# A spectral filter with a gated feed-forward branch: the gate and up products of the last row block as seven block products, and the schedule written anew

## The chip, the cores and the metric

The kernel runs on one core of a Trainium2 chip. A core has TensorE (PE, matrix products), VectorE (DVE), ScalarE (ACT), GpSimd (POOL) and SyncE (SP, which issues most transfers); each works through its own queue in the order in which it was written, and waits on semaphores for the others. Matrix products leave their sums in PSUM, from which VectorE and ScalarE read. The metric is the device time of one execution in microseconds, as the median of several runs.

## The reference

```python
xn = _layernorm(x, axis=-1)              # x: 2048 rows of 512
X = rfft2(xn); y = irfft2(X * (w_r + 1j * w_i), (S, D))      # s
gate = einsum("bsd,df->bsf", xn, W_gate) # 512 -> 1376
up   = einsum("bsd,df->bsf", xn, W_up)
h = gate * (gate > 0) * up
g = silu(einsum("bsf,fd->bsd", h, W_down))
return x + s * g
```

So there are two branches over the same normalised rows: a two-dimensional Fourier filter (s) and a feed-forward branch whose output is a gate (g). All values are 32-bit.

## The kernel before

Every 32-bit operand of a product is split into a high and a low 16-bit part, and each product is made in three passes (high by high, high by low, low by high; the list is PASSES). The 2048 rows stand as 16 tiles of 128. Eight chunks of two tiles (index c or q, 0 to 7) carry the loading and the Fourier branch; four row blocks of 512 rows (c = 0 to 3) carry the feed-forward branch. The 1376 features are 11 tiles (index f): ten of 128 and a last one of 96.

For a row block and a feature tile `product` makes gate or up: 12 matmuls of 128 weights by 512 rows (four slices of the 512 inputs, three passes) into a PSUM tile gu{c}_{f}_{0 or 1}. `rectify` (ScalarE) takes the positive part of gate into r, `hidden` multiplies it with up on VectorE (h32), takes the high part on ScalarE and the low part on VectorE (h16). `down` adds three matmuls of one feature tile to the PSUM tile dn{c}_{i} of row tile i; `gate` makes g from it on ScalarE. `weights` of the products are loaded in seven groups (`load_group`), scaled and split (`group_split`) in the first 60 us or so. The scale of the down weights needs the greatest value over all partitions, which goes to DRAM and back (row_md, rows_md).

The Fourier branch of a chunk is a chain over all engines: fold and split (eo, ee, xs), first stage (s, t), to DRAM (A_d), back with rows exchanged (at), then y, a, xx, the filter (xsp, tt on VectorE, po and pf as sums of tt on POOL, p), z, v, again to DRAM (C_d) and back (ct), a second stage s2 (zz on ScalarE, ae on POOL, ye and sv on VectorE). `finish` multiplies sv with g, adds the rows of x that were loaded again (xt) and stores out.

All steps are given to the class `Plan` with their engine, an estimated cost, what they read and write, and for some a due time. Plan's `run` walks in its own estimated time, gives every engine the most urgent step whose inputs are there, counts tiles of each kind of buffer (k4, k2, xg, gu, dn and so on), and so sets the order in which each engine's instructions are written. The order is then kept by the chip; the estimates are used for nothing else. The due times of the Fourier stages are the lists at the head of the file (FIRSTS, MIDS, LASTS); those of the products come from a running clock (`tick`). From `ff_steps`: a down step follows its product by six feature tiles.

Of the kernel before, what the change touches and what calls it, by code (L numbers as in the profile page):

```python
# [14 lines left out]
P = 128  # L15
# [10 lines left out]
TAIL = NFT - 1  # L26

# [5 lines left out]
T0, DOWN, FILTER, TICK = 1.2, 93.937, 134.179, 1.169  # L33
FIRSTS = [53.32, 98.69, 53.46, 108.61, 118.2, 143.13, 197.12, 178.58]
MIDS = [150.3, 160.34, 188.08, 192.0, 219.21, 237.31, 253.81, 275.45]
STAGES = [0, 12.12, 20.71, 25.24]
LASTS = [286.02, 290.71, 285.79, 312.67, 324.45, 353.1, 333.77, 342.56]
ENDS = [21.7, 8.89]
LOADS, LOADX = [-0.52, -0.11, 3.18, None, None, None, None], [-30, -0.3]
FOLDS, FOLD_LEAD, MARGIN = ['DVE', 'DVE', 'DVE', 'DVE', 'DVE', 'DVE', 'DVE', 'DVE'], 97.974, 1.95  # L40
HIGH_ACT = {(0, 1), (2, 1), (0, 0), (3, 1), (2, 0), (3, 0)}
NORM, TURN1 = (('DVE', 'ACT'), ('DVE', 'ACT')), 'PE'
YCOST, VCOST, SCOST, MODE, JOIN = 0.63, 0.59, 0.6, 0.095, 21.31
BUSY, LATE = 42, 0.4
SQUARES, HALF = 43.857, 2
HURRY, SLOW, SLOW_TO = -2.352, 1, 20
LOWS = [("DVE", "DVE")] * 8
ALONE, EVAC, WHOLE = (((0,), (1,)), ((0, 1),)), ("ACT", "DVE"), .95
HALVES, HEADS, STATS = ('gu', 'F'), [None, 13.67], ((0, 1),)
RATE, SLACK, TURNKB = 320, .6, 1300  # L50
LEADS = [None, 6.55, 6.95, 7.64, 6.43, 6.38, 7.22]
# [29 lines left out]
class Plan:  # L81
# [47 lines left out]
    def run(self):  # L129
        steps = self.steps  # L130
        for s in reversed(steps):
            s.due = 1e9 if s.due is None else s.due
            for d in s.deps:
                t = s.due - d.cost - d.lag
                d.due = t if d.due is None else min(d.due, t)
        base = lambda n: n[0] if isinstance(n, tuple) else n
# [9 lines left out]
        dma, todo, order, mode = 0., {e: [] for e in free}, [], 0  # L146
# [7 lines left out]
        for _ in steps:  # L154
            best = None
            for e, mine in todo.items():
# [16 lines left out]
                if at:  # L173
# [9 lines left out]
                    if best is None or t < best[0]:  # L183
                        best = t, s
# [13 lines left out]
            if s.kb:  # L198
                if s.block:
                    s.end = free[e] = max(s.end, dma + s.block)  # L200
                dma = max(dma, s.end) + s.kb / (340 if t < 40 else RATE)
                s.end = dma + (SLACK if t > 40 else 0.)
            if s.port:
                ports[e] = s.end
# [32 lines left out]
def pool(n):  # L237
    return .26 + n / 600
# [7 lines left out]
def kernel(ctx: ExitStack, tc: tile.TileContext, x, wg, wu, wd, wl, ew, sp, c_r, c_d, c_m, c_x, c_s, out):  # L246
# [14 lines left out]
    E_d = dram.tile([2, 2, 1024], F32, name="E_d")  # L261

# [6 lines left out]
    wgu = [wpool.tile([P, 2, 2, 4, P * sum(f < TAIL for f in g)], F16, name=f"wgu{i}") for i, g in enumerate(GROUPS)]  # L269
    wgt = wpool.tile([P, 4, 3, P], F16, name="wgt")  # L270
# [7 lines left out]
    md = cpool.tile([P, NFT + 1], F32, name="md")  # L278
    sc = cpool.tile([P, NFT], F32, name="scd")
# [11 lines left out]
    T = Plan({"k4": 12, "k2": 10, "h16": NFT, "xg": NBL + 1, "F": 2, "gu": 2, "dn": 2, "q": 4, "q4": 2, "mv": 4, "m": 4, "p": 4, "am": 1, "mid": 3})  # L291
# [34 lines left out]
    def stats(c, q, j):  # L326
# [6 lines left out]
        tile_of(f"mv{c}", "mv", [P, 2, 2], F32)  # L333
        if c == 0:
            tile_of(f"xf{c}", "k4", [P, 2, D + 2], F32)
        for i in range(2):
            if (c, i) in STATS:
# [38 lines left out]
    def deviations(cs):  # L376
# [15 lines left out]
        step("DVE", 2.4, run, reads=[(f"mv{c}", i) for c in cs for i in range(2)], writes=[(name, 2)], port=True)  # L392

    def normalise(c, q, at, engines=("DVE", "DVE")):
# [3 lines left out]
        def run(i):  # L398
            to, x = T[f"xf{c}"][:, i, 0:D], T[f"x{c}"][:, i, :]
            if engines[i] == "ACT":  # L400
                ACT.activation(to, x, AF.Identity, bias=T[q][:, 0, i:i + 1], scale=at()[:, i:i + 1])
            else:
                DVE.tensor_scalar(to, x, T[f"mv{c}"][:, i, 0:1], at()[:, i:i + 1], op0=ALU.subtract, op1=ALU.mult)
        for i in range(2):
            e = engines[i]
            step(e, .62 if e == "ACT" else dve2(512), lambda i=i: run(i), reads=[*x_names(c, i), (f"mv{c}", i), (q, 2, i) if c < 2 else (q, 2)],
                 writes=[(f"xf{c}", i)], port=e == "DVE")

    def turn(c, lows):
# [844 lines left out]
```

## Time and profile before

| | us |
|---|---|
| runs shown, median (lowest to highest of 3) | 407.4 (406.66 to 407.64) |
| the profiled execution | 406.56 |
| its span, first to last instruction | 404.8 |
| busy: TensorE | 398.4 (98%) |
| busy: VectorE | 305.0 (75%) |
| busy: ScalarE | 190.8 (47%) |
| busy: GpSimd | 50.4 (12%) |
| moved by DMA | 51.79 MB |

The trace is of one execution. A group of its rows is one kind of instruction: output and inputs by the program's names, shape, count, then the busy time and the mean duration of one in ns, then the time that the engine idled ahead of it and who ended that. For TensorE the mean duration holds the pipeline's latency and is not the pace; the pace is read from the chain of work that ended last, where a piece is its start, its length and the count of its instructions. The profile's page cuts the span into 40 slices of 10.1 us; another view gives each engine's busy time between two times. All rows of helper functions bear one line number.

### The profile page before, as it was taken

To read this page: it belongs to the slowest core of one execution; us is meant where nothing else is said; L and a number is where in the kernel's file an instruction comes from. 1 tells how busy PE (TensorE), PEld (TensorE's weight loads), DVE (VectorE), ACT (ScalarE), POOL (GpSimd) and SP (SyncE) were. 2 spreads that over 40 slices of the span, in tenths; PEclk is the share of its full clock that TensorE was granted. 3 is DMA by queue.
4 is the path that set the end of the run, shared out by engine and by line. 5 is a ranking of instruction groups with operands and counts; after the bars stand their busy time and mean duration, and the time that the engine had idled before them with its cause. 6 is when DMAs were issued, how large, how long until landed. Compare 5 with 4: busy or idle time off the path is not lost.

```text
span 404.8 us, 7658 instructions
## 1 busy us (share of the span) xinstructions
PE 398.4 (98%) x3004; PEld 211.2 (52%) x3004; DVE 305.0 (75%) x656; ACT 190.8 (47%) x368; POOL 50.4 (12%) x72
## 2 busy tenths in 40 slices
PE   8999999999999999999999999999999999999996
PEld 7854445444444444455565455546555445544446
DVE  4989898998699998327867568787872326889874
ACT  6989753454566753131444435424533236451211
POOL 0000000000000000004212014030330006516000
PEclk9999999999999999999999999999999999999999
DMA  7992000352099967930006450172102498433342
GB/s 256 401 324 80 0 2 7 105 108 101 12 276 289 278 33 201 255 119 2 2 0 187 162 160 2 25 223 95 51 5 52 122 237 215 157 104 106 104 157 104
DMA packets 36436, 51.79 MB, mean 128 GB/s; under 512 B 15856, under 2 KB 17744, under 8 KB 36400
## 3 DMA queue, kind: packets, MB, share of 16 engines
q1 hardware_dynamic: 36400, 51.31, 44.0%
q8 instruction: 23, 0.38, 0.4%
q14 instruction: 13, 0.11, 0.1%
HBM read 35.55 MB, written 12.60 MB: 119 GB/s over the span
## 4 chain that ended last, share of the span: by engine, by line
PE 89%; DMA 5%; DVE 4%; ACT 1%; issue 0%; POOL 0%; DVEq 0%
PE gu L74 49%; PE dn L74 28%; PE z L74 3%; PE xx L74 3%; PE s L74 3%; DMA row_md<-md 2%; DMA x<-in_x 2%; PE y L74 2%; PE v L74 2%; DMA rows_md<-row_md 1%; PE dn_3bb L74 0%; PE dn_3b L74 0%; ACT wgu L74 0%; DVE eo L74 0%; ACT xT L74 0%; DVE xT L74 0%
## 5 line engine op out<-in xcount | busy, mean ns | idle before, releaser
L74 PE MATMUL gu<-xT,wgu 128*128 128x512 f16 (+1 forms) x960 | 208.3, 374 | 1.1 <-DVE h L74 0.6
L74 PEld LDWEIGHTS <-wgu 128*128 128x128 f16 x960 | 93.0, 98 | 107.2 <-issue 3.9
L74 PE MATMUL dn<-wds,h 128*128 128x512 f16 (+2 forms) x528 | 116.0, 373 | 0.5 <-DVE wds L74 0.5
L74 PEld LDWEIGHTS <-h 128*128 128x128 f16 (+1 forms) x594 | 54.3, 98 | 57.9 <-issue 3.0
L74 ACT ACTIVATE h<-h 128x512 f16<-128x512 f32 (+1 forms) x44 | 27.4, 627 | 58.5 <-DVE h L74 58.4
L74 DVE TENSOR_TENSOR h<-gu,r 128x512 f32<-128x512 f32 (+3 forms) x52 | 33.1, 636 | 27.1 <-PE gu L74 25.3
L74 POOL TENSOR_TENSOR po<-tt,tt 128x256 f32<-128x256 f32 x16 | 13.8, 864 | 262.5 <-DVE tt L74 249.1
L74 ACT ACTIVATE r<-gu 128x512 f32<-128x512 f32 (+2 forms) x44 | 25.7, 583 | 38.4 <-PE gu L74 35.6
L74 DVE TENSOR_TENSOR h<-h,h 128x512 f16<-128x512 f32 (+1 forms) x44 | 29.9, 696 | 7.1 <-ACT h L74 7.0
L74 POOL TENSOR_TENSOR ae<-zz 128x128 f32<-128x128 f32 (+1 forms) x32 | 21.2, 696 | 49.9 <-ACT zz L74 39.6
L74 DVE SCALAR_TENSOR_TENSOR tt<-xsp,cw,wt 128x512 f32<-128x512 f32 x32 | 25.9, 864 | 0.0
L74 ACT ACTIVATE g<-dn,cdi 128x512 f32<-128x512 f32 (+1 forms) x16 | 10.6, 672 | 25.5 <-PE dn L74 25.5
L74 DVE TENSOR_TENSOR z<-z,z 128x1024 f16<-128x1024 f32 x8 | 9.8, 1223 | 11.0 <-ACT z L74 11.0
L74 PE MATMUL gu<-xT,wgt 128*64 128x256 f16 (+1 forms) x144 | 17.0, 310 | 0.0
L74 DVE TENSOR_TENSOR a<-y,a 128x1024 f16<-128x1024 f32 x8 | 9.8, 1219 | 8.7 <-ACT a L74 8.7
L74 DVE TENSOR_TENSOR t<-v,t 128x1024 f16<-128x1024 f32 x8 | 9.7, 1219 | 8.6 <-ACT t L74 8.6
L74 POOL TENSOR_TENSOR pf<-tt,tt 128x256 f32<-128x256 f32 x16 | 14.8, 941 | 4.9 <-issue 3.6
L74 DVE TENSOR_TENSOR sv<-sv,g 128x512 f32<-128x512 f32 (+2 forms) x18 | 11.0, 648 | 5.3 <-ACT g L74 5.2
L74 DVE SCALAR_TENSOR_TENSOR wgu<-raw,p,wgu 128x512 f16<-128x512 f32 x20 | 14.2, 746 | 0.8 <-ACT wgu L74 0.7
L74 ACT ACTIVATE a<-y 128x1024 f16<-128x1024 f32 x8 | 8.1, 1022 | 13.8 <-PE y L74 13.8
L74 ACT ACTIVATE z<-z 128x1024 f16<-128x1024 f32 x8 | 8.2, 1021 | 13.3 <-PE z L74 13.3
L74 DVE TENSOR_TENSOR p<-pf,p 128x1024 f16<-128x1024 f32 x8 | 9.8, 1225 | 5.6 <-ACT p L74 5.6
(151 smaller groups left out, 447.2 us busy)
## 6 DMA issues: line engine op xcount, KB each, us to landing
A_d<-t SPq DMA_DIRECT2D x16, 256.0 KB, 4.3
rw<-in_wl SPq DMA_DIRECT2D x8, 512.0 KB, 5.2
wt<-in_wl SPq DMA_DIRECT2D x8, 512.0 KB, 4.9
at<-A_d SPq DMA_DIRECT2D x8, 512.0 KB, 4.2
C_d<-t SPq DMA_DIRECT2D x16, 256.0 KB, 3.2
ct<-C_d SPq DMA_DIRECT2D x16, 256.0 KB, 6.8
xt<-in_x SPq DMA_DIRECT2D x16, 256.0 KB, 4.1
out<-xt SPq DMA_DIRECT2D x15, 256.0 KB, 2.1
```

What stands on the lines that cost most here:

```text
L74: return lambda *args, **kw: self.tc.keep_in_program_order(f(*args, **kw))
```

## The change

For the last row block, four of the five pairs of feature tiles ((0, 1), (5, 6), (7, 8) and (2, 9)) no longer make 2 × 2 products of 12 matmuls by 512 rows. Their gate and up, taken as a product of 2 by 2 blocks (two halves of the rows, two halves of the inputs), come from seven block products of 12 matmuls by 256 columns, `mult` in `fast_products`. Three PSUM tiles (A, B, C; sa, sb, sc by name) hold partial sums; ScalarE copies A to B and C to `back` (sk), VectorE adds B and back to C and E (se). The rest is as in rectify and hidden, on half-row tiles h16_3_n_m.

This needs sums of weight blocks and of row blocks. `weight_sums` loads the raw weights of a pair again, scales them on ScalarE, makes four differences on VectorE, splits them (wT), and writes one of them over part of the up weights in wgu. `row_sums` makes four sums of the normalised rows of block 3, splits them and sends them through DRAM to be transposed (xS).

Beside that: the normalised rows of chunks 4 to 7 go through DRAM to their transpose (X_d) instead of straight from on-chip memory. g of blocks 0 to 2 goes to DRAM (G_d) and is loaded again in `finish`. In `finish`, chunks 0, 1, 3 and 4 copy x to out in DRAM and add s times g to it with an accumulating transfer that POOL issues; the others load xt and add on VectorE as before. The row statistics of chunks 2 and 4 to 7 go to ScalarE; more high parts of weights too (HIGHS); half of POOL's sums go to VectorE (SUM2, DIFF2). There are fewer buffers of most kinds (ROOM) and three for gu. Feature tiles go in pairs, with the down steps two pairs behind, and single rows of down in block 0. The planner's costs and all due times are new.

```diff
-T0, DOWN, FILTER, TICK = 1.2, 93.937, 134.179, 1.169
-FIRSTS = [53.32, 98.69, 53.46, 108.61, 118.2, 143.13, 197.12, 178.58]
+T0, DOWN = 1.2, 98.707
+FIRSTS = [31.43, 109.07, 105.79, 129.3, 181.09, 150.51]
...
+PAIRS = ((0, 1), (3, 4), (5, 6), (7, 8), (2, 9))
+STATS, ADDS, COPIES = ['DVE', 'DVE', 'ACT', 'DVE', 'ACT', 'ACT', 'ACT', 'ACT'], ['DMA', 'DMA', 'DVE', 'DMA', 'DMA', 'DVE', 'DVE', 'DVE'], [105.83, 259.66, 138.19, 267.03, 599.36, 405.66, 358.32, 606.44]
+SUM2, DIFF2 = ['POOL', 'POOL', 'DVE', 'POOL', 'DVE', 'DVE', 'POOL', 'DVE', 'POOL', 'DVE', 'DVE', 'POOL', 'POOL', 'DVE', 'DVE', 'POOL'], ['DVE', 'POOL', 'POOL', 'POOL', 'POOL', 'DVE', 'DVE', 'DVE', 'POOL', 'DVE', 'POOL', 'DVE', 'POOL', 'DVE', 'DVE', 'POOL']
+ROOM = {"k4": 10, "k2": 8, "kg": 4, "cm": 3, "h16": 11, "xg": 3, "F": 2, "gu": 3, "dn": 1, "q": 4, "q4": 2, "mv": 4, "m": 4, "p": 4, "am": 1, "mid": 3}
-    T = Plan({"k4": 12, "k2": 10, "h16": NFT, "xg": NBL + 1, "F": 2, "gu": 2, "dn": 2, "q": 4, "q4": 2, "mv": 4, "m": 4, "p": 4, "am": 1, "mid": 3})
+    T = Plan(ROOM)
...
-            SP.dma_start_transpose(xt.rearrange("p i k r -> p (i k) r"), x16().rearrange("p i h d -> p (i h d)"))
+            SP.dma_start_transpose(xt.rearrange("p i k r -> p (i k) r"), x16().rearrange("p i h d -> p (i h d)") if DIRECT[c] else X_d[c])
...
+    def weight_sums(n, due):
...
+                step("SP", .5, lambda i=i, j=j, of=of, o=o: SP.dma_start(T[raw][:, i, :, j * P:j * P + P], of[:, :, o:o + P]),
+                     reads=["go"], writes=[(raw, i, j)], lead=8, kb=330, due=due - 12)
+                part = lambda i=i, j=j: T[raw][:, i, :, j * P:j * P + P]
+                step("ACT", act(512) + .1, lambda part=part, f=f, i=i: ACT.activation(part(), part(), AF.Copy, scale=csc[:, i, f:f + 1]),
+                     reads=[("csc", f)], writes=[(raw, i, j)])
...
+        minus((0, 0), (1, 0), (0, 0), G + U, t1)
+        minus((1, 0), (1, 1), (1, 0), U + [t1], t3)
+        minus((1, 1), (1, 1), (0, 0), U + [t1, t3], t2)
+        minus((0, 1), (0, 1), (1, 1), G + [t2], t4)
...
+    def fast_products(c, n):
...
+        def mult(to, x, w, fresh, reads):
+            def run():
+                for j in range(2):
+                    for k in range(2):
+                        for p, (h, l) in enumerate(PASSES):
+                            matmul(T[to][:, j, :], w(h, k, j), x(l, k), start=fresh and j == k == p == 0, stop=j == k == 1 and p == 2, skip_group_check=True)
+            step("PE", pe(12, 256), run, reads=reads, writes=[to, "turn"], due=tick(pe(12, 256)), margin=FMARGIN)
...
+        mult(A, rows(0, 0), plain(0, 0), True, X[0] + W[0])
+        copy(B, A)
+        mult(C, rsum(2), plain(1, 0), True, [(f"xS{c}", 1)] + W[1])
+        copy(back, C)
+        mult(B, rsum(1), summed(2), False, [(f"xS{c}", 0)] + U(2, 3))
+        mult(A, rows(0, 2), plain(0, 2), False, X[0] + W[0])
+        rect(r1, A)
+        add(C)
+        mult(B, rsum(0), summed(0), False, [(f"xS{c}", 0)] + U(0, 1))
+        mult(C, rows(1, 2), summed(1), False, X[1] + U(0, 1))
+        rect(r2, C)
+        add(E)
+        mult(B, rsum(3), plain(1, 2), False, [(f"xS{c}", 1)] + W[1])
+        step("DVE", dve(512), lambda: DVE.tensor_mul(T[r1], T[B], T[r1]), reads=[B], writes=[r1], due=clock[0] + 3)
...
     def finish(c, i, due):
...
+            step("SP", .5, lambda: SP.dma_start(T[g], G_d[:, 2 * c + i, :]), reads=[("G_d", b, j), (sn, 2)], writes=[(g, 0)], lead=8, kb=256)
+        if ADDS[c] == "DMA":
+            to = out[:, 2 * c + i, :]
+            step("SP", .5, lambda: SP.dma_start(to, x[:, 2 * c + i, :]), writes=[("out", c, i)], lead=10, kb=400, due=COPIES[c])
+            step("DVE", dve(D), lambda: DVE.tensor_mul(T[sn][:, i, :], T[sn][:, i, :], T[g]), port=True,
+                 reads=[(g, 0), *((sn, k) for k in range(3))], writes=[(sn, 3 + i)])
+            step("POOL", 1.2, lambda: POOL.dma_start(to, T[sn][:, i, :], accum_op=ALU.add), reads=[(sn, 3 + i)], writes=[("out", c, i)], kb=512, lag=3., due=due)
+            return
```

The written order shows what this does around two places. The first is VectorE in row block 2, after the product gu2_6_1 (h32 and h16 are the hidden rows, p16 and z16 the Fourier stages). Before:

```order
L74 TENSOR_TENSOR pf_4_3091<-po_4_3126 128x4x32
L74 TENSOR_TENSOR z16_3_3142<-z3_3101,z16_3_3142 128x1024 [waits Activation_49]
L74 TENSOR_TENSOR p16_4_3149<-pf_4_3091,p16_4_3149 128x1024 [waits Activation_49]
L74 TENSOR_TENSOR h32_2_7_3165<-gu2_7_1_3129,r2_7_3082 128x512 [waits PE_49]
L74 TENSOR_TENSOR h16_2_6_3098<-h32_2_6_3095,h16_2_6_3098 128x512
L74 TENSOR_TENSOR h16_2_7_3168<-h32_2_7_3165,h16_2_7_3168 128x512 [waits Activation_49]
```

After, at the same products, on VectorE (rp2 is the raw weights of the third of the weight sums):

```order
L87 TENSOR_TENSOR pf_2_3129<-tt2_2_3095,tt3_2_3098 128x8x32
L87 TENSOR_TENSOR h32_2_6_3153<-gu2_6_1_3041,r2_6_3016 128x512 [waits PE_49]
L87 TENSOR_TENSOR z16_4_3148<-z4_3101,z16_4_3148 128x1024 [waits Activation_49]
L87 TENSOR_TENSOR p16_2_3157<-pf_2_3129,p16_2_3157 128x1024 [waits Activation_49]
L87 TENSOR_TENSOR h32_2_7_3180<-gu2_7_1_3135,r2_7_3127 128x512 [waits PE_49]
L87 TENSOR_TENSOR h16_2_5_3001<-h32_2_5_2997,h16_2_5_3001 128x512
L87 TENSOR_TENSOR h16_2_6_3162<-h32_2_6_3153,h16_2_6_3162 128x512 [waits Activation_49]
L87 TENSOR_TENSOR rp2_3074<-rp2_3074 128x512 [waits Activation_49]
L87 TENSOR_TENSOR h16_2_7_3186<-h32_2_7_3180,h16_2_7_3186 128x512 [waits Activation_49]
```

The reading of gu2_6_1 (h32_2_6) and the low part h16_2_5 have moved behind the sums of another chunk's filter, and the differences of the weights stand between the low parts.

The second place is ScalarE in row block 3, near the end of the products. Before:

```order
L74 ACTIVATE ye4_4295<-ae4_4292 128x2 [waits Pool_49]
L74 ACTIVATE r3_9_4552<-gu3_9_0_4522 128x512 [waits DMAHW5_49,DMAHW1_49,PE_49]
L74 ACTIVATE sv4_4554<-ye4_4295 128x4 [waits DVE_49]
L74 ACTIVATE h16_3_8_4557<-h32_3_8_4549 128x512 [waits DVE_49]
L74 ACTIVATE h16_3_9_4599<-h32_3_9_4596 128x512 [waits DVE_49]
L74 ACTIVATE ye5_4493<-ae5_4482 128x2 [waits Pool_49]
L74 ACTIVATE r3_10_4610<-gu3_10_0_4581 96x512 [waits PE_49,Activation_49]
```

After, on ScalarE (sq3_4 is the positive part of C of the last fast pair, h16_3_4_0 and h16_3_4_1 its hidden rows; DMASW are transfers that POOL issued):

```order
L87 ACTIVATE ye6_4936<-zz6_4903 128x2 [waits DMASW5_49,DMASW4_49]
L87 ACTIVATE sq3_4_4938<-sc3_4_4761 128x512 [waits DVE_49,PE_49]
L87 ACTIVATE ae7_4953<-zz7_4912 128x2 [waits DMAHW6_49,DMAHW2_49,Activation_49]
L87 ACTIVATE ae7_4953<-zz7_4912 128x2
L87 ACTIVATE ye7_4956<-zz7_4912 128x2 [waits DMAHW3_49]
L87 ACTIVATE ye6_4936<-ae6_4928 128x2 [waits Pool_49]
L87 ACTIVATE h16_3_4_0_4970<-sr3_4_4858 128x512 [waits DVE_49]
L87 ACTIVATE h16_3_4_1_4977<-se3_4_4926 128x512 [waits DVE_49]
```

The steps of the last fast pair now stand behind a step that waits for two accumulating transfers.

More of the change, by code (lines that the diff above doesn't have):

```diff
@@ L593, in rhos @@
         def rhos():
+            for i in range(2):
+                DVE.tensor_copy(csc[:, i, fs[0]:fs[-1] + 1], T[f"p{g}"][:, 0, i:2 * nf:2])
             inverse_of(T[f"p{g}"][:, :, :2 * nf])
@@ new lines, in down @@
+        cost = pe(3, cols.stop - cols.start)
+        step("PE", cost, run, reads=[("wd", f), ("wdl", f), (h16, 0), (h16, 1)] + ["turn"] * (f == 0 and i > 0), writes=[name], due=tick(cost))
+    def gate(c, i, part=0):
+        name, g, cols = f"dn{c}_{i}" + "b" * part, f"g{c}_{i}", columns(c, i)[part]
+        if g not in T.tiles:
+            tile_of(g, "k2", [P, D], F32)
+        step("ACT", act(cols.stop - cols.start) + .1, lambda: ACT.activation(T[g][:, cols], T[name], AF.Silu, scale=cdi),
+             reads=[name, "scd"], writes=[(g, part)], due=clock[0] + 4)
+        if c < NBL - 1:
+            step("SP", .6, lambda: SP.dma_start(G_d[:, 4 * c + i, :], T[g]), reads=[(g, 0)], writes=[("G_d", c, i)], kb=256)
@@ L1114 @@
         hidden(0, f)
-    for rows in ((0, 1), (2, 3)):
+    for i in range(4):
         for f in range(NFT):
-            down(0, f, rows)
-        for i in rows:
-            gate(0, i)
+            down(0, f, i)
+        gate(0, i)
     for c in range(1, NBL):
+        for n in range(len(PAIRS)):
+            if PLAINS[5 * c + n] == "fast" and PLAINS[5 * c - 5 + n] == "plain":
+                weight_sums(n, TPREP + n * TSTEP)
         ff_steps(c)
```

338 lines of the change are left out of this document (236 added, 102 removed).

## The prediction

> **What bounds the kernel now.** I read the page's busy rows and slices first, then the chain that ended last, then TensorE's groups apart by shape, then the busy time by stretches of 20 us, then the DMA issues.
>
> ```profile
> span 404.8 us, 7658 instructions
> PE 398.4 (98%) x3004; PEld 211.2 (52%) x3004; DVE 305.0 (75%) x656; ACT 190.8 (47%) x368; POOL 50.4 (12%) x72
> ...
> PEclk9999999999999999999999999999999999999999
> DMA  7992000352099967930006450172102498433342
> ...
> 57.29 7.71 DMA row_md<-md
> 65.01 4.73 DMA rows_md<-row_md
> ...
> 206.63 1.31 PE xx L74 x12
> 207.93 2.59 PE gu L74 x12
> ...
> 214.96 1.29 PE dn L74 x6
> ...
> 221.43 1.34 PE z L74 x24
> ...
> 227.95 0.77 PE v L74 x12
> ...
> 237.04 5.18 PE gu L74 x24
> ...
> 401.38 0.38 ACT g L74
> 401.78 0.30 DVE sv L74
> 402.10 0.29 DVE xt L74
> ```
>
> TensorE is busy 398.4 of 404.8 us at full clock. Of the 6.4 us that it lacks, 3.4 lie behind its last matmul, which ends as g begins at 401.4; the other 3 are in the head and before the first down product, for which the chain waits through row_md and rows_md. So time can come only from less TensorE work, and be lost only where another engine lets it wait. VectorE, at 75%, is the one with the least to spare.
>
> The sum is made against the profiled execution: span 404.8, run 406.56, hence 1.76 us around the span. The median of the runs shown, 407.4, is 0.84 us above that run, so my figure for the median is the span forecast plus 2.6 us. Differences under 0.3% (1.2 us) I call no change.
>
> **The products.** A plain pair of feature tiles is four products of 12 matmuls over 512 columns. The chain has two of them in 5.18 us, 215.8 ns a matmul, so 10.36 us a pair. A fast pair is seven products of 12 matmuls over 256 columns, each with its own weight load. Before has that shape in xx: 12 in 1.31 us, 109 ns each.
>
> ```profile
> L74 PE MATMUL gu<-xT,wgu 128*128 128x512 f16 x912 | 202.4, 379 | 0.0
> L74 PE MATMUL xx<-a,cD 128*128 128x256 f16 x96 | 11.8, 273 | 0.0
> L74 PEld LDWEIGHTS <-p 128*128 128x128 f16 x192 | 11.3, 98 | 2.1 <-ACT h L74 0.4
> ```
>
> Seven times 1.31 is 9.17 us, a gain of 1.19 us per pair and 4.8 us for four. The 36 more weight loads per pair I cost at nothing, since the running matmuls cover them: xx has a load before each matmul and stays at 109 ns, and z, with 192 loads of 98 ns for its 192 matmuls over 128 columns, does 24 in 1.34 us, 56 ns each (first fence). The 1.31 us of xx is from inside a stream of gu products, where the fast pairs stand too. The sum loses nothing elsewhere on TensorE: the other counts are the same.
>
> The Trainium skill, "TensorE: Matmul & The Clock Gate", Part 3, under "What overlaps and what doesn't", says that a weight load overlaps a running matmul only when it goes to another group of rows. By that rule the 98 ns loads would stand in front of every 256-column matmul; xx and z, with a full-height load each, disagree. It is a rival below.
>
> **What the fast pairs ask of the other engines.** These are durations of VectorE's steps (ScalarE's for 512 elements is in the fence behind them).
>
> ```profile
> L74 DVE TENSOR_TENSOR h<-h,h 128x512 f16<-128x512 f32 x40 | 27.2, 698 | 6.2 <-ACT h L74 6.1
> L74 DVE TENSOR_TENSOR h<-gu,r 128x512 f32<-128x512 f32 x38 | 26.1, 687 | 22.8 <-PE gu L74 22.1 <-ACT r L74 0.4
> L74 DVE SCALAR_TENSOR_TENSOR tt<-xsp,cw,wt 128x512 f32<-128x512 f32 x32 | 25.9, 864 | 0.0
> ...
> L74 DVE TENSOR_TENSOR pf<-po 128x128 f32<-128x128 f32 x32 | 10.5, 387 | 0.0
> L74 DVE BATCH_NORM_STATS2 st<-x 128x6 f32<-128x512 f32 x15 | 10.1, 675 | 3.3 <-DMA x<-in_x 3.3
> L74 DVE TENSOR_TENSOR xt<-xt,sv 128x512 f32<-128x512 f32 x15 | 10.0, 718 | 0.0
> ...
> L74 DVE TENSOR_TENSOR p<-pf,p 128x1024 f16<-128x1024 f32 x8 | 9.8, 1225 | 5.6 <-ACT p L74 5.6
> ...
> L74 DVE TENSOR_TENSOR xs<-eo 128x256 f32<-128x256 f32 x16 | 6.1, 419 | 0.0
> ```
> ```profile
> L74 ACT ACTIVATE h<-h 128x512 f16<-128x512 f32 x40 | 24.9, 628 | 51.4 <-DVE h L74 51.3
> ```
>
> VectorE, by these rows:
> - weight_sums for four pairs: each 4 subtractions (0.70), low parts of 1024 and 512 columns (1.22 + 0.70) and two of 256 (about 0.4): 5.5, together 22.
> - row_sums: 4 × 0.70 + 2 × 1.22 = 5.2.
> - Two adds of back per fast pair (8 × 0.69): 5.5. The other steps of hidden stay as many as before.
> - Half of POOL's sums moved over, 16 of 256 and 16 of 128 elements (0.42, and 0.39 as pf): 13.
> - Off it: ten chunk halves' statistics (10 × 0.675, with their small aggregations about 8.5), eight adds of xt (5.7), four high parts and four normalisations (at most 0.69 each; I take 4).
> - Small steps for means and scales: an estimate of +4.
>
> Sum about +31: 305 becomes 336 of some 402 us, 84%. ScalarE gains some 75 steps of mostly 0.63 us (scaling and splitting weights, statistics, copies of A and C), about 47 us, and stays under 60%; POOL loses about 22. As averages all fits. The stretches decide:
>
> ```profile
> core 0: us, PE busy (x) PEld busy (x) DVE busy (x) ACT busy (x) POOL busy (x), PEclk, DMA share, GB/s
> 0.00:20.00 20.00, 18.19 (x146) 16.17 (x147) 14.02 (x47) 16.23 (x43) 1.00 (x8) 1.00 0.91 327
> ...
> 80.00:100.00 20.00, 20.00 (x94) 9.01 (x93) 18.81 (x41) 10.14 (x13) 0.00 (x0) 1.00 0.44 106
> ...
> 220.00:240.00 20.00, 20.00 (x214) 10.86 (x213) 10.19 (x14) 8.03 (x12) 0.00 (x0) 1.00 0.62 203
> 240.00:260.00 20.00, 20.00 (x188) 11.14 (x186) 18.03 (x29) 9.49 (x14) 7.42 (x8) 1.00 0.01 2
> ...
> 300.00:320.00 20.00, 20.00 (x128) 9.34 (x127) 6.65 (x8) 7.32 (x9) 0.00 (x0) 1.00 0.21 53
> 320.00:340.00 20.00, 20.00 (x176) 9.96 (x174) 6.18 (x10) 9.11 (x24) 6.52 (x15) 1.00 0.98 233
> 340.00:360.00 20.00, 20.00 (x162) 9.85 (x164) 18.58 (x34) 7.18 (x19) 6.30 (x6) 1.00 0.34 110
> ```
>
> - **Head.** DMA is already 0.91 full. The later raw loads now stand behind other loads, and the weights of group 4 come about when they are wanted. Cost 0 to 1.5 us; I take 0.4.
> - **First down product.** The chain row_md, rows_md (12.4 us) starts a few us earlier by the written order, and the first down product is wanted a little earlier too. It had 0.5 us of stall; between 0 and 2 us, I take no change. If writes ahead of row_md in SP's queue are slow, this goes up first.
> - **80 to 100 us.** VectorE is full before (18.8 of 20) and stays so. What is late next is the products of block 1; I take +0.5, between −0.8 (split steps stand earlier) and +1.5.
> - **220 to 260 us.** VectorE had 28.2 of 40; it gets most of the moved POOL sums and the second pair's weight sums. From the end of gu2_5_1 to the start of gu2_8_0 TensorE now has four products (10.36), v, xx, dn and z (0.77 + 1.31 + 1.29 + 1.34): 15.1 us. In that time VectorE has written h32_2_5 and all rows to h32_2_6: two steps of 0.69, five tt (4.3), six sums of 256 (2.5), eight of pf (3.1), two of 1024 (2.4), three of xsp (about 1.1) and a wait of some 0.4 for the copy of v: 15.2. gu2_8_0 takes over the tile that h32_2_6 reads (three tiles of that kind), so there is no slack: 0 to 2 us, I take 0.5.
> - **300 to 374 us, the fast pairs.** VectorE has most room here (6.7 and 6.2 of 20): about 40 of 67 us with its new steps. In a pair each copy (0.63) or add (0.69) stands beside one product of 1.31 or a down step of 0.65 before TensorE touches that tile again, so it is hidden if its engine is free, and costs its overhang, up to 0.7 us, if not. 0 to 3 us over four pairs; I take 0.4.
> - **Fewer buffers.** The rows of down products of block 0 go one by one, in turn on two kinds of tile; a gate step (0.38 for the quarter row at the end) has the next row's 33 matmuls, 7.1 us, as cover. The smaller pools of on-chip tiles show as waits of loads on VectorE's last reads; SP's queue is in order, so a g load that waits for sv also holds the xt loads behind it. They are written 8 us or more ahead of use; I take 0, up to 2 if that cover is gone.
> - **Tail.** After the last fast product TensorE has some 24 us of down products; VectorE about 22 us of work. The closing chain (g, sv, xt, out) is as before: 0.
>
> **The transfers.** x and g through DRAM, the sums' transposes and the weight reloads add about 14 MB to 51.8.
>
> ```profile
> A_d<-t SPq DMA_DIRECT2D x16, 256.0 KB, 4.3
> C_d<-t SPq DMA_DIRECT2D x16, 256.0 KB, 3.2
> ct<-C_d SPq DMA_DIRECT2D x16, 256.0 KB, 6.8
> ...
> out<-xt SPq DMA_DIRECT2D x15, 256.0 KB, 2.1
> ...
> xT<-x SPq DMA_TRANSPOSE x6, 5.8
> ```
>
> They are issued 8 us and more ahead of use, against 2.1 to 6.8 us for their kinds, and the slices show idle DMA. A transpose that reads DRAM isn't in this trace: between the 5.8 us of one from on-chip memory and that plus a read of 6.8, 12.6 us; I take 8, hidden by a lead of some 14 us. Nor is an accumulating transfer: between out's 2.1 us and twice ct's, 13.6, as it reads its target too; I take 4.3, A_d's. (The Trainium skill, "DMA: Bandwidth & Descriptors", section "Anatomy of one DMA — SWDGE (gpsimd) path", gives about 2.0 us plus bytes over 436 GB/s; for 256 KB that is an estimate of 2.6 us, and nothing here shows it.) Its cover: ScalarE's step ye6 waits for chunk 4's two accumulations, and behind it in ScalarE's queue stand sq3_4 and h16_3_4_0, which TensorE's last down products of row 0 want. Between the multiply that frees the first of these transfers and that point stand 13 steps of VectorE, 6.5 us. At 4.3 us nothing is late; above about 6.5, each us is TensorE's.
>
> **The sum.** −4.8 + 0.4 + 0.5 + 0.5 + 0.4 = −3.0: span 401.8, median 404.4.
>
> **The rivals.**
> - *VectorE falls behind in 220 to 260 us (slower).* For: 15.2 us against 15.1 of cover, and every step stands in order, so a late row carries on to the hidden rows, to gu's tiles and to TensorE. Against: 220 to 240 had 9.8 us of idle VectorE, and by the written order the backlog drains by 260. It decides once VectorE's load there exceeds TensorE's 40 us by more than what is won. If the steps of two pairs of weight sums (11 us) and all of POOL's 7.4 fall into it, 28.2 + 18.4 = 46.6 of 40: 404.4 − 0.5 + 6.6 = 410.5.
> - *Weight loads stand alone.* If each of the 36 added loads of a pair costs its 98 ns, that is 3.5 us a pair and 14 in all: 404.4 + 14 = 418.4 (all 84 loads would make it 437). xx at 109 ns and z at 56 speak against it.
> - *Accumulations land late.* At 13.6 us the wait at ye6 is 7.1 us: 411.5. For: POOL issues these and the row has no precedent here. Against: no 256 KB row above takes longer than 6.8.
> - *The gain is eaten.* Stalls near the upper ends in half of the stretches, about 4.8 us, leave 406.2 to 408.6.
>
> **How the numbers follow.** The forecast (402 to 406.1): 0.56; eaten within 1.2 us of 407.4: 0.10; VectorE behind: 0.19; accumulations or other transfers late: 0.10; loads alone: 0.02; better than 402 (no stall at all gives 402.6, with the earlier splits about 401.5): 0.03. Faster 0.59, same 0.10, slower 0.31. To leave out no more than 2 in 10 the range goes from 401.5 to 411.5; the forecast's own range is 402 to 406.1.
>
> **What would show it.** Right: fast products of about 1.31 us in the chain, TensorE busy near 394, VectorE near 335, no single wait of TensorE over 1 us. Wrong: sb or sc products above 1.5 us (loads alone); waits of gu for VectorE in block 2 (behind); ScalarE's ye steps waiting for out (late accumulations); the first down product later than 73 us (the chain through row_md). The forecast fails most simply if several of the places I call free by under 1 us aren't.

## The result, and the profile after

The changed kernel takes 404.62 us in the median of nine runs (402.83 to 406.70), the kernel before 407.40 on the same chip: a ratio of 0.9942, 95% interval 0.9917 to 0.9967. On a second chip it was 403.18 against 406.08, 0.9924 (0.9910 to 0.9937). The profiled execution took 403.82 us with a span of 402.0, 2.8 us shorter than the span before.

The page after:

```profile
span 402.0 us, 8180 instructions
...
PE 394.6 (98%) x3148; PEld 225.4 (56%) x3148; DVE 324.1 (81%) x731; ACT 232.2 (58%) x458; POOL 31.8 (8%) x48
...
DMA packets 53367, 66.50 MB, mean 165 GB/s; under 512 B 20752, under 2 KB 30832, under 8 KB 53328
```

TensorE is busy 3.8 us less, VectorE 19 us more, ScalarE 41 more, GpSimd 19 less; 14.7 MB more are moved. In the chain of work that ended last, a fast pair (the second of the four) reads as follows; each line is a start, a length, an engine with its output tile, and a count of matmuls:

```profile
337.68 1.31 PE sa L87 x12
338.99 1.31 PE sc L87 x12
340.30 1.31 PE sb L87 x12
341.61 1.31 PE sa L87 x12
342.92 0.65 PE dn L87 x3
343.57 1.31 PE sb L87 x12
344.88 1.31 PE sc L87 x12
346.19 0.65 PE dn L87 x3
346.84 1.31 PE sb L87 x12
```

Each product takes the 1.31 us of xx, and no hand-over between the engines shows a gap. The next two fences show what TensorE waited for, before and then after (engine, tile and line, who ended the wait, us in total, times, the longest):

```profile
PE small L74 <- DVE md L74: 1.1, 1, 1.1
PE gu L74 <- DVE h L74: 0.6, 1, 0.6
PE gu L74 <- DVE xT L74: 0.5, 1, 0.5
PE dn L74 <- DVE wds L74: 0.5, 1, 0.5
```

```profile
PE gu L87 <- ACT r L87: 1.8, 1, 1.8
PE small L87 <- DVE md L87: 1.1, 1, 1.1
PE gu L87 <- DVE h L87: 0.6, 1, 0.6
PE dn L87 <- ACT g L87: 0.3, 1, 0.3
```

After, the last of these ends at 93.4 us. So the losses lie ahead of 110 us, and they can be counted: up to there both kernels have done the same number of matmuls of every other kind, and differ only in how many gu matmuls are done. Groups of TensorE in 0 to 110 us, before and after:

```profile
L74 PE MATMUL gu<-xT,wgu 128*128 128x512 f16 x227 | 49.9, 379 | 0.0
```

```profile
L87 PE MATMUL gu<-xT,wgu 128*128 128x512 f16 x217 | 47.8, 379 | 1.8 <-ACT r L87 1.8
```

After is ten matmuls of 0.216 us behind, 2.2 us. From 110 us on, before needs 404.8 − 110 = 294.8 us; after needs 402.0 − 110 = 292.0 and does 2.2 us more work in it, so with the same work 289.8. The change gains 5.0 us behind 110 us and loses 2.2 ahead of it. I call that corrected time "the rest from 110 us". For any kernel here it is span − 110 − (227 − gu matmuls done) × 0.216.

The larger part of the loss is one story. The fences show a wait of ScalarE, SP's issues around 54 us, and a transfer in the chain that ended last, all after:

```profile
ACT x L87 <- DMA A_d<-t: 5.0, 1, 5.0
```

```profile
54.00 0.64 SPq L87 DMA_DIRECT2D A_d<-t  x1
54.73 0.54 SPq L87 DMA_DIRECT2D row_md<-md  x1
55.31 0.68 SPq L87 DMA_DIRECT2D A_d<-t  x1
64.14 0.32 SPq L87 DMA_DIRECT2D rows_md<-row_md  x1
```

```profile
55.31 9.58 DMA A_d<-t
```

The second A_d write lands 9.58 us after its issue, against 4.1 in the median of all sixteen. The tile that it reads is wanted next by ScalarE's high part of x. Behind that step in ScalarE's queue stands r, and TensorE waits 1.8 us for r.

### The profile page after: what moved, and what is told of

Same layout as the page of the kernel before. It is cut to its first block, busy times and chain, and to the rows that moved or that the text cites. A ratio compares the mean times of both kernels' runs of the same rounds, so it can differ in the third digit from the quotient of the medians.

```text
span 402.0 us, 8180 instructions
## 1 busy us (share of the span) xinstructions
PE 394.6 (98%) x3148; PEld 225.4 (56%) x3148; DVE 324.1 (81%) x731; ACT 232.2 (58%) x458; POOL 31.8 (8%) x48
## 4 chain that ended last, share of the span: by engine, by line
PE 85%; ACT 9%; DMA 2%; DVE 1%; issue 1%; SPq 0%; ACTq 0%
PE gu L87 34%; PE dn L87 27%; PE sb L87 4%; ACT wgu L87 4%; PE s L87 3%; PE z L87 3%; PE sa L87 3%; PE xx L87 3%; PE sc L87 3%; DMA A_d<-t 2%; PE y L87 2%; PE small L87 2%; PE v L87 2%; ACT wds L87 1%; ACT r L87 1%; ACT xf L87 1%
## 5 line engine op out<-in xcount | busy, mean ns | idle before, releaser
L87 PE MATMUL gu<-xT,wgu 128*128 128x512 f16 (+1 forms) x768 | 165.3, 372 | 2.4 <-ACT r L87 1.8
L87 ACT ACTIVATE h<-h 128x512 f16<-128x512 f32 (+1 forms) x36 | 22.0, 624 | 29.5 <-DVE h L87 29.5
L87 DVE TENSOR_TENSOR h<-gu,r 128x512 f32<-128x512 f32 (+3 forms) x44 | 27.6, 627 | 11.6 <-PE gu L87 8.6
L87 ACT ACTIVATE r<-gu 128x512 f32<-128x512 f32 (+2 forms) x36 | 20.7, 578 | 21.2 <-PE gu L87 18.2
L87 POOL TENSOR_TENSOR tt<-tt,tt 128x256 f32<-128x256 f32 x8 | 8.6, 1076 | 253.6 <-DVE tt L87 224.1
L87 DVE TENSOR_TENSOR h<-h,h 128x512 f16<-128x512 f32 (+1 forms) x36 | 23.8, 684 | 1.9 <-ACT h L87 1.8
L87 ACT ACTIVATE g<-dn,cdi 128x512 f32<-128x512 f32 (+1 forms) x16 | 10.8, 672 | 19.0 <-PE dn L87 17.4
L87 PEld LDWEIGHTS <-wT 128*128 128x128 f16 x144 | 13.9, 98 | 3.1 <-issue 0.4
L87 DVE TENSOR_TENSOR t<-s,t 128x896 f16<-128x896 f32 (+1 forms) x16 | 10.6, 686 | 4.7 <-ACT t L87 4.7
L87 PEld LDWEIGHTS <-wgt 128*64 128x64 f16 (+1 forms) x144 | 9.7, 106 | 6.1 <-issue 0.8
L87 ACT ACTIVATE wgu<-raw 128x512 f16<-128x512 f32 x20 | 12.3, 620 | 0.0
```

Of the source, the lines that this page charges most:

```text
L87: return lambda *args, **kw: self.tc.keep_in_program_order(f(*args, **kw))
```

## The experiments

Names of steps that are used below: s is a product of the Fourier branch's first and last stage, with zz and ye behind it in the last; xt holds rows of x loaded again for the closing add.

First a table of all. The times of one row are from one chip, and the ratio is against the kernel before on that chip. The last three columns are from one profiled execution.

| kernel | median us | ratio (95%) | span | gu done at 110 us | rest from 110 us |
|---|---|---|---|---|---|
| before (first trace) | 407.40 | 1 | 404.8 | 227 | 294.8 |
| changed (first trace) | 404.62 | 0.9942 (0.9917 to 0.9967) | 402.0 | 217 | 289.8 |
| again | 403.18 | 0.9924 (0.9910 to 0.9937) | 401.4 | 220 | 289.9 |
| row_later | 402.81 | 0.9915 (0.9901 to 0.9928) | 400.9 | 223 | 290.0 |
| plain4 | 408.76 | 1.0061 (1.0048 to 1.0074) | 407.6 | 216 | 295.2 |
| plain_store | 402.17, one run | | 400.4 | 225 | 290.0 |
| no_prep | 404.16 | 0.9942 (0.9928 to 0.9957) | 402.2 | 218 | 290.3 |
| row_twice | 403.77 | 0.9930 (0.9916 to 0.9945) | 402.1 | 219 | 290.4 |
| row_act (its profiled execution took 405.99) | 403.87 | 0.9936 (0.9919 to 0.9952) | 404.2 | 207 | 289.9 |
| pe_max_kept | 402.50 | 0.9895 (0.9879 to 0.9912) | 400.7 | 224 | 290.1 |
| pe_max_silu | 401.66 | 0.9878 (0.9863 to 0.9893) | 400.1 | 227 | 290.1 |
| fast5 | 419.98 | 1.0331 (1.0316 to 1.0346) | 418.0 | 221 | |
| adds_dve | 415.79 | 1.0231 (1.0217 to 1.0244) | 414.2 | 221 | |
| pe_max | 419.82 | 1.0333 (1.0315 to 1.0351) | 420.0 | 229 | |

The last column is left out for three kernels whose new order lost 12 us and more. It says most: 289.8 to 290.4 for every kernel that keeps the changed kernel's order and its fast products, whatever else is edited, and 295 for the two without them.

**again.** No edit.

> The changed kernel once more, unedited. Five of its nine executions so far had a granted clock of 0.999 to 1.000 and took 402.8 to 404.6 us, four had 0.996 and took 405.8 to 406.7. Theory A (the lower clock follows a wait of TensorE inside the kernel, the one of 1.8 us at 64 us being the longest): again both groups, 2 us apart. Theory B (a state of the chip at the time of the first measurement): one group only. Median expected 404.3, between 403 and 406.

Five runs lie between 402.96 and 403.46, at a granted clock of 0.999 or 1.000; TensorE's wait for r is 1.3 us here. That is one group only, which spoke for theory B until row_act (below) showed what the other group probably is.

**plain4.** The fast products alone undone.

```diff
-PLAINS = ['plain', ..., 'plain', 'fast', 'plain', 'fast', 'fast', 'fast']
+PLAINS = ['plain'] * 20
```

> All pairs of the last row block by plain products again: the fast products, the sums of weights and rows and their loads go; x and g through DRAM, the accumulations, the buffers and the due times stay. The planner writes the order anew from those. Theory A (the fast products are what wins; all else is about even): +4.2 us of products against the changed kernel's chain (sa, sb and sc pieces there add to 37.2 us, the plain 41.4), less nothing, since TensorE waits for nothing that the sums delay: 408 to 409. Rival B (VectorE's extra steps eat part, and the rearrangement around gains): 405 to 407. Rival C (the other parts lose): over 410.

408.76 is 5.6 us above the changed kernel and 2.7 above before. By the last column the products make 5.3 us of it (295.2 against 289.9). The loss ahead of 110 us plain4 shares with the changed kernel (216 gu matmuls there against 220). So all else that the change does costs some 2.7 us, and the fast products win it back twice. That is theory A in kind, with the other parts worse than even. (The planner wrote a new order here too, but 295.2 is within 0.4 us of what before needs, so nothing in it went astray.)

**no_prep.** The weight and row sums stay planned, so all else keeps its place, but are not written; the fast products read plain weights and rows, which makes the last row block's gate and up wrong.

```diff
-            s.fn()
+            if not s.skip:
+                s.fn()
...
+                T.skip = True
                 weight_sums(n, TPREP + n * TSTEP)
+                T.skip = False
```

> The steps of weight_sums and row_sums stay in the plan, so the order of all others is the changed kernel's, but their instructions, loads and transposes are left out; the fast products read plain weights and rows in their place, so the last row block's gate and up are wrong. VectorE loses about 27 us of work. Theory A (TensorE waits for nothing that these steps delay: in the trace of the changed kernel it has no wait after 94 us): within 0.6 us of the changed kernel's 403.2 on that chip. Rival B (they cost something that the list of waits doesn't show): 1 us or more faster, where row block 2 is between 220 and 260 us.

VectorE falls from 324.1 to 299.8 us busy, and nothing is gained: 290.3 from 110 us on. The 24 us of sums are hidden whole. This is also the answer on row block 2: between 220 and 260 us VectorE has 33.6 us of 40 in the changed kernel (14.92 and 18.68), and TensorE waits for nothing there.

The median is 1.0 us above the changed kernel's 403.2, more than the 0.6 that theory A allowed, but to the slower side, which rival B can't explain. Part of it lies in the head: at 45 us the trace is already three gu matmuls (0.65 us) behind that of the run again, long before the first step that is left out. What this has to do with the edit is open.

**plain_store.** The eight accumulating transfers as plain stores, so out of chunks 0, 1, 3 and 4 lacks x.

```diff
-            step("POOL", 1.2, lambda: POOL.dma_start(to, T[sn][:, i, :], accum_op=ALU.add), ...
+            step("POOL", 1.2, lambda: POOL.dma_start(to, T[sn][:, i, :]), ...
```

> The eight accumulating transfers become plain stores that POOL issues, so out of chunks 0, 1, 3 and 4 lacks x. Accumulating ones took 7.0 us from issue to landing (median), SP's plain stores of the same size 2.1. Theory A (reading the target and adding is what costs): 3 us or less. Rival B (POOL's way of issuing, about 1 us of POOL each, and the traffic there are what cost): 6 to 7 us stay. The time within 0.5 us of the changed kernel's in both, since TensorE doesn't wait for them.

DMA issues (KB each, median us to landing), the changed kernel and then plain_store:

```profile
out<-sv POOLq DMA_DIRECT2D x8, 256.0 KB, 7.0
...
out<-xt SPq DMA_DIRECT2D x7, 256.0 KB, 2.1
```

```profile
out<-sv POOLq DMA_DIRECT2D x8, 256.0 KB, 4.5
```

The result lies between both theories: accumulating costs 2.5 us, and a plain store issued by POOL still takes 2.4 us longer than SP's. For the time neither counts, since the rest from 110 us is 290.0. The single run is 1.0 us below the changed kernel, outside the 0.5 that was expected; that comes from the stretch ahead of 110 us (225 gu matmuls done against 220, which is 1.1 us). In the changed kernel ScalarE's ye steps wait 3.7 us for these transfers, as the prediction feared, but not long enough to make TensorE wait.

**row_later.** row_md goes behind both A_d writes in SP's queue.

```diff
         order.sort(key=lambda k: k[0])
+        row = next(k for k in order if k[1].engine == "SP" and "row_md" in k[1].names)
+        i = order.index(row)
+        j = next(n for n in range(i + 1, len(order)) if order[n][1].engine == "SP")
+        order.insert(j, order.pop(i))
```

> SP's transfer row_md is issued behind both A_d writes of chunk 2's first stage, not between them; nothing else moves. Theory A (row_md, 128 single elements, took 7.7 us alone in the kernel before, and the A_d write queued behind it took 9.6 instead of 4.1; ScalarE waited 5.0 us for that landing and TensorE 1.8 for ScalarE): the second A_d lands in about 4 us, ScalarE waits under 1 us, TensorE's wait at 64 us is gone, row_md begins 0.7 us later; time -1.5 us (-1.8 +0.3), and if the lower clock comes from that wait, no execution at 0.996. Rival B (the A_d write is slow by itself or by other traffic): it stays at 8 us or more, TensorE's wait stays within 0.5 us, time 0 to +0.7.

ScalarE's 5 us wait for A_d is gone, as theory A has it. Little of the gain comes through. SP's issues, and some of what TensorE still waits for in row_later:

```profile
54.22 1.27 SPq L87 DMA_DIRECT2D A_d<-t  x2
55.53 0.66 SPq L87 DMA_DIRECT2D row_md<-md  x1
63.25 0.33 SPq L87 DMA_DIRECT2D rows_md<-row_md  x1
```

```profile
PE gu L87 <- ACT r L87: 0.6, 1, 0.6
...
PE dn L87 <- ACT g L87: 0.3, 1, 0.3
```

The wait of gu for r is now at 71 us: r stands behind ScalarE's split of the down weights, which waits for the scale from rows_md. One wait took the other's place, and the −1.5 us expected became −0.4.

**row_twice and row_act.** What holds A_d up? First the single elements sent twice, then sent by ScalarE's queue.

```diff
+            if name == "md":
+                SP.dma_start(spare.rearrange("a p -> p a"), col)
             SP.dma_start(row.rearrange("a p -> p a"), col)
```

> The changed kernel in its own order with row_md's 128 single elements sent twice, once to a spare row ahead of the true one. Theory A (those elements hold up the A_d write behind them one to one): A_d lands some 8 us later, ScalarE's wait goes from 5 to about 13 us, TensorE's at 64 us from 1.3 to about 9, and after some 4 us of waiting the granted clock falls to half, as it did in the kernels with waits of 6 us, and comes back some 4 to 8 us after the work does: +10 to +13 us, mean clock about 0.985. Rival B (A_d is slow for another reason): under +1.5 us, clock 0.999.

No change: A_d takes 8.6 us, TensorE waits 1.5. Two such transfers, one behind the other, held the write up no longer than one, and theory A's "one to one" falls.

```diff
-        step("SP", .6, lambda: SP.dma_start(row.rearrange("a p -> p a"), col), ...
+        step("SP", .6, lambda: (ACT if name == "md" else SP).dma_start(row.rearrange("a p -> p a"), col), ...
```

> The changed kernel in its own order, with row_md issued by ScalarE on a queue of its own instead of by SP between the two A_d writes. Sent twice, row_md held A_d up no longer than once (8.6 us against 9.0 to 9.6), so the hold-up is not a matter of how many elements there are. Theory A (what counts is the place in SP's queue): A_d lands in about 4 us, ScalarE's wait at 60 us is gone and TensorE's falls from 1.3 to about 0.6, as with row_md behind A_d; time -0.4 us, about 0.9915. Rival B (the single-element writes hold up what shares the transfer engines, whichever queue issues them): A_d stays at 8 us or more, TensorE's wait at 1.2 us or more, time within 0.3 us of the changed kernel.

```profile
54.60 10.77 DMA A_d<-t
```

This is rival B. ScalarE issued row_md at 54.16 us, ahead of the second A_d write, and that write lands after 10.77 us although row_md is in another queue. So the hold-up is not a matter of SP's queue. (The Trainium skill, "Trainium Kernel Development and Optimization", section "Key Constraints", says that transfers from the queues of SP, ScalarE and GpSimd run on the same 16 engines and interleave. This run agrees, in so far as a transfer of one queue held up one of another.) What exactly makes the large write wait for small ones that were issued ahead of it stays open.

The profiled execution of row_act was a longer one, 405.99 us at a mean clock of 0.996, and it shows what that is. TensorE's matmuls around 64 us in row_act, then in the changed kernel (start, length, count, and the idle time ahead):

```profile
66.65 4.44 PE L87 MATMUL gu<-xT,wgu 128*128 128x512 f16 x12 [2.38 <-ACT r L87]
```

```profile
66.16 2.75 PE L87 MATMUL gu<-xT,wgu 128*128 128x512 f16 x12 [1.81 <-ACT r L87]
```

and row_act's busy time and granted clock (third from the right) by stretches:

```profile
64.00:66.00 2.00, 0.26 (x2) 0.00 (x0) 0.00 (x0) 0.52 (x1) 0.00 (x0) 1.00 0.07 22
66.00:67.00 1.00, 0.35 (x2) 0.19 (x2) 0.37 (x1) 1.00 (x3) 0.00 (x0) 1.00 0.07 23
67.00:68.00 1.00, 1.00 (x5) 0.36 (x3) 1.00 (x3) 0.71 (x2) 0.00 (x0) 0.54 0.00 0
68.00:69.00 1.00, 1.00 (x4) 0.36 (x3) 0.93 (x4) 0.00 (x0) 0.00 (x0) 0.50 0.00 0
69.00:70.00 1.00, 1.00 (x3) 0.29 (x2) 0.52 (x4) 0.42 (x1) 0.00 (x0) 0.50 0.00 0
70.00:71.00 1.00, 1.00 (x4) 0.25 (x2) 0.00 (x0) 0.30 (x1) 0.00 (x0) 0.76 0.00 0
71.00:72.00 1.00, 1.00 (x26) 0.70 (x26) 0.81 (x2) 0.02 (x1) 0.00 (x0) 1.00 0.00 0
```

A wait of 2.38 us was followed by half clock for about 3.5 us, and the next product took 1.69 us longer. So a wait that was 0.6 us longer cost 2.3 us. Half clock for 3.5 of 404 us is a mean of 0.996.

**pe_max, pe_max_kept, pe_max_silu.** The greatest value without the way through DRAM.

```diff
+            step("DVE", .2, lambda: DVE.tensor_scalar(rows(), unit, col, None, op0=ALU.mult), ...
+            step("PE", .3, lambda: matmul(T["top_md"], ones, rows(), start=True, stop=True), ...
+            step("DVE", .22, lambda: DVE.tensor_reduce(top, T["top_md"], axis=AX.X, op=ALU.max), ...
```

> The greatest value for the down weights' scale no longer goes to DRAM and back (row_md 7.7 to 8.3 us, rows_md 2.8 to 4.7): VectorE multiplies the unit matrix with md (128 by 128), TensorE spreads it over all partitions in one product with ones, VectorE takes the maximum from PSUM. The rest is the changed kernel, planned anew. Theory A (this chain, with the A_d write held up behind row_md, makes TensorE's waits at 64 and 71 us, 1.3 to 1.8 us, and most of what the first 110 us lose): the waits go, time -1.3 to -2.0 us, 401.2 to 401.9. Rival B (the wait of 1.3 us is another's, or VectorE's full load there gives a new wait): between -0.5 and +0.5.

This kernel is 13.5 us slower than before, though the stretch ahead of 110 us became the best of all by the gu products (229 matmuls, no wait for r). The planner had written a new order for the whole kernel, and in the last row block TensorE waited 6.8 us for se and twice, 5.9 us together, for zz. So this run doesn't answer what it was for. In pe_max_kept the order is the changed kernel's, with only these steps put in their place (the spreading matrix lies in a weight tile that is free then):

```diff
+        moved = [(at + 3, ("PE", self.spread)), (at + 5, top[1]), (at + 5.01, scales[1])]
+        order = [k for k in order if k[1] not in (spread[1], top[1], scales[1]) and k[1].tag != "row_md"] + moved
```

> The greatest value for the down weights' scale by TensorE (unit matrix times md, spread by a product with ones, maximum from PSUM), this time with the written order of the changed kernel kept: only row_md and rows_md go, one product comes in behind the next gu products, and the maximum and the scale steps move up on VectorE. Theory A (row_md, by holding up the A_d write behind it, and the late scale make TensorE's waits at 64 and 71 us): no wait of gu for ScalarE there, -1.3 to -1.9 us against the changed kernel, about 0.988 of the kernel before. Rival B (VectorE's full load in 67 to 98 us turns the gain into waits of dn or s later, before 110 us): 0 to -0.6, about 0.992.

0.9895: the waits for r are gone, and the ratio is 1.2 us better than that of the run again, so theory A holds nearly in full. It also confirms who held A_d up: without row_md the write lands after 3.3 us. The next edit moves ScalarE's table load, which takes 1.28 us ahead of the first g:

```diff
+        moved.append((at + 8, ("ACT", self.table)))
...
+    T.table = lambda: ACT.activation(warm, ones[:, 0:1], AF.Silu)
```

> As the kernel before this in the list, and a one-element Silu on ScalarE at about 62 us of the plan, so that the table load of 1.28 us ahead of the first g (at 91 us in the changed kernel, where TensorE waits 0.3 us for g) is done while ScalarE is less busy. Expected a further -0.3 us if that wait is TensorE's own, 0 if the next wait takes its place; +0.5 or more if the early table load holds up a step that TensorE wants.

401.66 us, 0.9878 (0.9863 to 0.9893): the fastest kernel here, ahead of before and of the changed kernel. TensorE's waits in it, and its gu products in 0 to 110 us:

```profile
PE small L87 <- DVE md L87: 1.1, 1, 1.1
PE gu L87 <- DVE h L87: 0.6, 1, 0.6
PE gu L87 <- DVE xTf L87: 0.2, 1, 0.2
```

```profile
L87 PE MATMUL gu<-xT,wgu 128*128 128x512 f16 x227 | 49.9, 379 | 0.0
```

The 2.2 us are back: 227 as before. The step from pe_max_kept is 0.84 us, more than the 0.3 expected. In the traces both kernels have done the same matmuls at 90 us, and at 100 us pe_max_silu is three dn matmuls (0.65 us) ahead, so the gain lies where the first g stands, and is larger than the 0.3 us in the list of waits.

**fast5 and adds_dve.** Two edits that let the planner write the order anew: the fifth pair fast too, and all adds of x on VectorE.

```diff
-PLAINS = [..., 'fast', 'plain', 'fast', 'fast', 'fast']
+PLAINS = [..., 'fast', 'fast', 'fast', 'fast', 'fast']
```

```diff
-STATS, ADDS, COPIES = ..., ['DMA', 'DMA', 'DVE', 'DMA', 'DMA', 'DVE', 'DVE', 'DVE'], ...
+STATS, ADDS, COPIES = ..., ['DVE'] * 8, ...
```

> The fifth pair of the last row block, (3, 4), is fast too; the planner writes the order anew. Its weight sums come at about 230 us, where I counted VectorE as full. Theory A (each fast pair is worth 1.2 us and what prepares it is hidden): -1.2 us against the changed kernel, 402.0. Rival B (220 to 260 us has no slack for 5.5 us more of VectorE): TensorE waits there for gu's tiles, 0 to +4 us.

> All chunks load xt and add on VectorE; no copy of x to out and no accumulating transfer; the planner writes the order anew. VectorE gets 8 adds, 5.7 us, GpSimd loses 8 issues of 1.05 us. Theory A (the accumulations bring room on VectorE that TensorE doesn't need at that place): within 0.6 us of the changed kernel. Rival B (VectorE is short at the end): 1 to 4 us slower, with waits of the down products for h16 after 365 us. Rival C (the accumulations' 7 us held something up): faster by 0.5 us or more.

Both lost far more than any theory had: 420.0 and 415.8 us. fast5's longest waits of TensorE, and busy times and granted clock (third from the right) around them:

```profile
PE sb L87 <- DVE se L87: 6.8, 1, 6.8
PE s L87 <- DMA ct<-C_d: 5.0, 2, 4.2
```

(In these rows the number behind the comma is TensorE's busy time, and the third of the busy times is VectorE's.)

```profile
352.00:356.00 4.00, 0.21 (x8) 0.00 (x0) 4.00 (x12) 1.83 (x7) 0.95 (x1) 1.00 1.03 238
356.00:360.00 4.00, 1.79 (x24) 1.25 (x25) 3.90 (x8) 2.21 (x8) 2.38 (x4) 0.66 0.91 332
360.00:364.00 4.00, 0.00 (x0) 0.00 (x0) 4.00 (x7) 1.50 (x5) 1.95 (x3) 0.50 0.61 205
364.00:368.00 4.00, 2.15 (x11) 1.49 (x11) 3.11 (x6) 0.63 (x1) 2.54 (x4) 0.50 1.01 203
```

VectorE is busy nearly all through while TensorE stands, and the clock falls to half. The waits are in the last row block. In fast5 VectorE's add se stood behind sv, ye and xt steps, and two more waits, 5.0 us together, ended with loads of ct. In adds_dve the longest wait, 6.3 us, is of a down product for h at 369 us, where rival B had put it, and the chain there has xt tiles with a store of 6.62 us and a load of 2.57 behind it. Between 200 and 300 us fast5 has one wait of 0.4 us, so the place that I had counted as full took 5.5 us more of VectorE. What a fifth pair is worth, and what the accumulations are worth in themselves, these runs don't tell, because the new order decided them.

## Why the prediction was right

The forecast was 404.4, and 404.62 was measured; the span was to shrink by 3.0 us and shrank by 2.8. Gain and loss are to be set apart in that: the gain came as worked out, the loss only in its sum.

- **The products:** −4.8 forecast, −5.0 by the rest from 110 us against before, −5.3 against plain4. The 1.31 us of xx was the right row for sa, sb and sc alike, and the loads' 98 ns cost nothing: the rival of weight loads that stand alone is out.
- **The stalls:** +1.8 forecast, +2.2 measured, but not where I had put them; that the two sums lie close together is luck. I gave 0.4 to the head, 0.5 to 80 to 100 us, 0.5 to 220 to 260 and 0.4 to the fast pairs. Measured: the head came out even (at 60 us 161 gu matmuls and 24 of s, 0.8 us, against 165 gu); 0.3 at 93 us for g; nothing in 220 to 260 and nothing in the fast pairs. About half a us ahead of 110 us is in no wait that the profile lists; some of it lies at the first g, by pe_max_silu, and the rest stays open. Of the prediction's own signs of being right, "no single wait of TensorE over 1 us" failed, with 1.8.
- **The step that failed** is "First down product ... I take no change". There lies 1.3 of the 2.2 us (1.8 against 0.5). I had the right transfers and the wrong direction: I feared that writes ahead of row_md would slow it, but row_md slowed the write behind it, and the price came through ScalarE's queue to a gu product and not to the down product. "Fewer buffers ... I take 0, up to 2" covers the mechanism, a step that waits for a tile until its store has landed; that the cut of k4 from 12 to 10 is what made ScalarE take that tile is argued, not tried.
- **The accumulations:** 4.3 us taken, 7.0 measured, above the 6.5 from which I had TensorE wait. It didn't: the ye steps waited, 2.6 us at the longest, and sq3_4 came in time. So a sign that I had named as one of being wrong came true without a price. The 6.5 us were worked out from VectorE's rows alone, without the idle time between them.
- **A transpose from DRAM:** 8 taken, 9.5 (8.4 on the second chip) measured; hidden, as forecast.
- **VectorE:** 336 forecast, 324 measured. Part of it is shorter steps, which a count at the old durations couldn't show: the 32 pf steps of 128 columns take 283 ns in the mean instead of 387 (3.4 us less), the tt steps 819 instead of 864 (1.4 us less). The sums for the fast products are 24.3 us by no_prep instead of 27.
- **The pinch in 220 to 260 us** (15.2 against 15.1 us) had no cost, and here is what was left of it. The second product of the first line is gu2_8_0, so it starts at 249.2; the second line is h32_2_6, done at 248.3:

```profile
246.63 5.34 PE L87 MATMUL gu<-xT,wgu 128*128 128x512 f16 x24
```

```profile
247.60 0.69 DVE L87 TENSOR_TENSOR h<-gu,r 128x512 f32<-128x512 f32 x1
```

TensorE took 15.2 us from the end of gu2_5_1, as forecast, and VectorE 14.2 instead of 15.2, although it also waited 0.6 us for POOL and 0.9 us for ScalarE in that time. One reason is that durations from the rows can't be added along a queue, since steps overlap a little: of two steps of 0.68 us the second starts 0.61 us behind the first.

```profile
360.85 0.68 DVE L87 TENSOR_TENSOR sv<-sv,g_0l 128x512 f32<-128x512 f32 x1
361.46 0.68 DVE L87 TENSOR_TENSOR sv<-sv,g_1l 128x512 f32<-128x512 f32 x1
```

There is some luck in the median too: four of the first nine executions had the lower clock and were some 2 us longer. Without them the first median would be 403.8.

## What to carry to other kernels

Count the matmuls done by a fixed time in both traces: that places a loss without any model, and shows which edits act where. When a written order comes from a planner, test an edit with the order kept; a new order is another kernel, and here it cost 12 to 17 us against the changed kernel in three of four cases. A small transfer of single elements can hold up a large one beside it, and the price appears on an engine that issued neither of them.

## What the runs showed of the hardware

- **A wait and the clock.** TensorE's clock stayed at 1.00 after waits of 1.3 to 1.9 us (again, row_twice, the changed kernel, plain4) and fell to half for about 3.5 us after one of 2.38 (row_act); in pe_max it fell likewise after one of 3.17. The Trainium skill, "TensorE: Matmul & The Clock Gate", section "What's actually happening", has the clock fall after an idle window of about 3.4 us; here a wait of 2.4 us was enough, and the time at half clock is near that length. So in these traces the edge lies between 1.9 and 2.4 us; whether the length of the wait alone decides isn't shown. The changed kernel's executions fall into two groups, 402.8 to 404.6 us at a clock of 0.999 to 1.000 and 405.8 to 406.7 at 0.996. That the four at 0.996 had such a wait is likely, since row_act shows it, but they left no trace.
- **Single elements.** 128 elements of 4 bytes took 7.2 to 9.4 us from their issue to the step that waited for them, sent once or twice, from SP's queue or ScalarE's, and a 256 KB write issued just behind landed after 8.6 to 10.8 us. In the changed kernel and its variants with the order kept the median of such writes was 3.5 to 4.1, and without the elements this one landed after 3.3 (pe_max_kept).
- **Accumulating to DRAM.** 256 KB from POOL took 7.0 us accumulating (7.3 on the second chip) and 4.5 plain, against 2.1 for SP's plain store.
